# The first loads across all partitions, and the first memories through two PSUM banks

## The chip, the cores and the metric

The kernel runs on one core of a Trainium2 chip. Its engines work side by side: TensorE (PE) for matmuls, VectorE (DVE), ScalarE (ACT), GpSimd (POOL), and SyncE (SP), which only issues transfers. Transfers between HBM and the on-chip memory run on 16 DMA engines that all queues share; here SP's and ACT's queues issue them. The metric is the device time of one execution in microseconds (us).

## The reference

Attention over a compressed memory, then a feed-forward block with a squared ReLU. For 8 batches and 8 heads, with 576 tokens, 64 channels and 32 memory slots:

```python
a = exp(phi - max(phi, over tokens));  a = a / (sum(a, over tokens) + 1e-9)
k_m = einsum('bhsm,bhsd->bhmd', a, k)
v_m = einsum('bhsm,bhsd->bhmd', a, v)
scores = q @ k_m.T / sqrt(64)
attn = softmax(scores);  x = attn @ v_m       # tokens x (heads x channels) = 4608 x 512
h = maximum(x @ w_in, 0)                      # w_in: 512 x 2048, 8-byte floats
out = (h * h) @ w_out                         # w_out: 2048 x 512, 8-byte floats
```

Sums and maxima over tokens don't depend on the order of the tokens, as long as phi, k and v keep the same one.

## The kernel before

The attention output is never formed: `attn @ v_m @ w_in` is computed as `attn @ u` with `u = v_m @ w_in`, once per batch and part of `w_in`. The feed-forward matmuls split each operand into a high and a low part, and so run three products each (lines 673 to 679 and 724 to 731).

The eight heads are two groups of four (`qd` 0 and 1, `NQ` = 2). phi lies in HBM as 576 rows of 256 numbers (two groups of 4 heads x 32 slots), k and v as 576 rows of 4 heads x 128 numbers per group. On chip the tokens lie on 128 partitions: four full chunks of 128 tokens and a fifth of 64, the tail. `e_sb` holds phi and later its exponentials, chunk by chunk.

For batch 0 everything starts at once, in an order written out by hand: the list `loads` issues the transfers, and the string `order` in line 958 says which piece of work is recorded next (`e` phi's exponentials, `m` the memories k_m and v_m, `d0` to `d3` the decoding of `w_in` from 8-byte floats, `a0` and `a1` scores and softmax, `u0` the first u). Each engine runs its own instructions strictly in the order in which they were recorded. A transfer takes one of eight semaphores in turn (DMAHW0 to DMAHW7), and the issue of one that takes a semaphore again waits until its last user has landed.

The pieces that the change and the prediction's steps touch:

- `first_phi` (line 903) calls `load_phi(0)`: chunks 0 to 3 on SP's queue, the 64-row tail on ACT's. `first_kv` (line 884) loads k and v of each group as two transfers of two chunks (`u_hi3` and `u_lo3`, `wo4` and `wo5`: rooms lent from later use) and a tail of 64 rows.
- `exp_phi` (line 166): DVE takes the maximum over chunks (L170, L175), TensorE transposes it (L180), DVE reduces (L185), TensorE spreads it (L190), DVE adds it (L199), ACT takes the exponential (L201).
- `memories` (line 322): DVE sums the exponentials (L332, L335), TensorE multiplies them with k and v, 20 matmuls per group (L350) and the sums (L357), DVE divides (L366 to L370), TensorE transposes (L377), DVE and ACT copy to `mem` one half of the partitions each (L385).
- `by_heads` (L408) makes the scores of `a0` from `mem`, then `first_softmax` (L487 to L519) runs on DVE and ACT; L497 is its exponential on ACT, L501 the sum after it. L677 are the first feed-forward matmuls.
- `decode` (L581, L584 on ACT; L586, L589, L594 on DVE; L601) turns pieces of `w_in` into 4-byte floats. `q` is loaded by L397, `w_in` by L568.
- `spin` (L149) issues matmuls whose result nobody reads; they keep TensorE going while it waits.

Of the kernel before, what the change touches and what calls it, by code (L numbers as in the profile page):

```python
# [8 lines left out]
F32 = mybir.dt.float32  # L9
# [3 lines left out]
AF = mybir.ActivationFunctionType  # L13
# [11 lines left out]
def attn_moe_kernel(ctx: ExitStack, tc: tile.TileContext, qT, kv, phi, w_in, w_out, outT):  # L25
# [16 lines left out]
    P = 128  # L42
# [16 lines left out]
    def rows(c):  # L59
        return min(P, S - c * P)  # L60
# [51 lines left out]
    def fill_all():  # L112
        for c in range(NCH):
            fill(c, kvb[c])
            if rows(c) < P:
                nc.gpsimd.memset(e_sb[rows(c):, c], 0.0)

    ones = const.tile([P, CW - 2 * D], F32, name="ones")
    nc.gpsimd.memset(ones, 1.0)
# [33 lines left out]
    def load_phi(b, nc_q=nc.sync):  # L153
        nfull = S // P
        assert b == 0 or ("read", b - 1) in ready
        nc.sync.dma_start(out=e_sb[:, :nfull], in_=phi[b, :nfull * P].rearrange("(c p) x -> p c x", p=P))
        if b > 1:
            for qd in range(NQ):
                nc_q.dma_start(
                    out=e_sb[D * qd:D * (qd + 1), nfull, :P], in_=phi[b, nfull * P:, qd * P:(qd + 1) * P]  # L160
                )
            return [e_sb[:, c] for c in range(nfull)] + [e_sb[:, nfull, :P]]
        nc_q.dma_start(out=e_sb[:rows(nfull), nfull], in_=phi[b, nfull * P:])
        return [e_sb[:rows(c), c] for c in range(NCH)]

    def exp_phi(b, e):

        w = NQ * P
        mx = one.tile([P, w], F32, name="phi_mx")
        nc.vector.tensor_tensor(out=mx, in0=e[0], in1=e[1], op=ALU.max)  # L170
        for x in e[2:]:
            n = x.shape[0]
            if fine and not starting:
                yield True
            nc.vector.tensor_tensor(out=mx[:n], in0=mx[:n], in1=x, op=ALU.max)  # L175
        yield
        ps = new_ps()
        tp, bc = bank(ps, 0), bank(ps, 1)
        for qd in range(NQ):
            nc.tensor.transpose(tp[:, qd * P:(qd + 1) * P], mx[:, qd * P:(qd + 1) * P], ident)  # L180
        if starting:
            spin(1, ident, k=2)
        yield
        nmx = work.tile([P, NQ], F32, name="nmx")
        nc.vector.tensor_reduce(  # L185
            out=nmx, in_=tp[:, :w].rearrange("p (q x) -> p q x", q=NQ), axis=AX.X, op=ALU.max, negate=True
        )
# [24 lines left out]

    def exp_phi_blocks(b, e):

        w = NQ * P
        nb = w // M
        mx = one.tile([P, w], F32, name="phi_mx")
        nc.vector.tensor_tensor(out=mx, in0=e[0], in1=e[1], op=ALU.max)
        for x in e[2:-1]:
            nc.vector.tensor_tensor(out=mx, in0=mx, in1=x, op=ALU.max)  # L220
        at = [(slice(D * qd, D * (qd + 1)), slice(P * qd, P * (qd + 1))) for qd in range(NQ)]
        for hs, cs in at:
# [17 lines left out]
        for hs, cs in at:  # L240
            nc.vector.tensor_tensor(out=e[-1][hs], in0=e[-1][hs], in1=mx[hs, cs], op=ALU.subtract)
        yield
        nfull = S // P
        nc.scalar.activation(e_sb[:, :nfull], e_sb[:, :nfull], AF.Exp)
        nc.scalar.activation(e[nfull], e[nfull], AF.Exp)
        ready.add(("phi", b))

    def load_kv(b, qd, lent=None):

        got = []  # L250
        for c in range(NCH):
            if lent:
                t = lent(c)
            elif qd and b > 1 and rows(c) < P:
                nc.sync.dma_start(out=kvb[c][D:, :, :2 * D], in_=kv[b, qd, c * P:])
                got.append(kvb[c])
                continue
            elif qd:

                name, bufs = ("tmp", 3) if c < 3 else ("low", 2)  # L260
                if b == 2 and c < 3:
                    if not c:
                        w1 = const.tile([P, 3, 4, CW], F32, name="w1")
                    t = w1[:, c]
# [10 lines left out]
            nc.sync.dma_start(out=t[:rows(c), :, :2 * D], in_=kv[b, qd, c * P:c * P + rows(c)])  # L275
            got.append(t)
        return got

# [43 lines left out]
    def memories(b, e, kvs, mem):  # L322
# [7 lines left out]
        if b == 0:  # L330
            total = one.tile([P, NQ * P], F32, name="phi_mx")
            nc.vector.tensor_tensor(out=total, in0=e[0], in1=e[1], op=ALU.add)  # L332
            for c in range(2, NCH):
                n = rows(c)
                nc.vector.tensor_tensor(out=total[:n], in0=total[:n], in1=e[c][:n], op=ALU.add)  # L335
# [33 lines left out]
        for qd in range(NQ):  # L369
# [3 lines left out]
                den[:, qd:qd + 1],  # L373
            )
        yield
        for i in range(2 * NQ):
            nc.tensor.transpose(  # L377
                tp[:, i * P:(i + 1) * P], kvn[:, i // NQ, i % NQ].rearrange("p a d -> p (a d)"), ident
            )
        if starting:  # L380
            spin(1, ident, k=3)
        yield
        for half, copy in ((0, nc.vector.tensor_copy), (1, nc.scalar.copy)):
            hs = slice(D * half, D * (half + 1))
            copy(mem[hs], tp[hs].rearrange("p (x r h m) -> p x r h m", x=2, r=NPAIR, h=2)[:, :, :, half])  # L385
        done_ps(ps)
        ready.add(("mem", b))

# [495 lines left out]
    def first_kv(qd):

        names = (("u_hi3", "u_lo3", "u_hi4"), ("wo4", "wo5", "wo6"))[qd]
        queues = ((nc.scalar, nc.sync, nc.scalar), (nc.sync, nc.sync, nc.scalar))[qd]
        got = []
        for name, nc_q in zip(names, queues):
            c = len(got)  # L890
            t = const.tile([P, 2, 4, 2 * D], F32, name=name)
            n = min(2, S // P - c)
            if n:
                x = kv[0, qd, c * P:(c + n) * P].rearrange("(c p) h x -> p c h x", p=P)
                nc_q.dma_start(out=t[:, :n], in_=x)
                got += [t[:, k] for k in range(n)]
            else:
                fill(c, t[:, 0])
                nc_q.dma_start(out=t[:rows(c), 0], in_=kv[0, qd, c * P:])
                got.append(t[:, 0])  # L900
        kvs[qd] = got
# [5 lines left out]
    def next_kv():  # L907
# [1 line left out]

    loads = [  # L910
        (first_phi,),
        (first_kv, 0),
        (first_kv, 1),
        (fetch_w_in, 0, 0),
        (task_q, 0, 0),
        (task_q, 0, 1),
# [314 lines left out]
```

## Time and profile before

| | us |
|---|---|
| median of 3 runs | 719.02 (718.85 to 719.22) |
| span of the profiled execution, first to last instruction | 717.0 |
| TensorE busy | 708.0 (99% of the span) |
| VectorE busy | 388.6 (54%) |
| ScalarE busy | 332.6 (46%) |
| GpSimd busy | 197.6 (28%) |

The profiled execution has no time of its own beside its span; the runs' median is 2.0 us above that span, which stands for what lies before the first and after the last instruction. Busy TensorE counts the `spin` matmuls too. The DMA engines are almost fully busy in the first three of the page's 40 slices (to 54 us) and far less in most of the others. In the rows "idle before" names what an engine stood waiting for; "SPq" and "ACTq" are the queues of instructions that issue transfers, q1 and q10 the packets that came from them. A time to landing runs from the start of the issue.

### The profile page before, as it was taken

What the parts mean: (1) busy time and instruction counts of PE and PEld (TensorE: products, weight loads), DVE (VectorE), ACT (ScalarE), POOL (GpSimd) and SP (SyncE); (2) the same over time, 40 slices, a digit from 0 to 9 for tenths busy, and PEclk for the clock granted to TensorE, in tenths of its full rate; (3) what the DMA queues carried; (4) which work ended last, traced back from release to release, by engine and by line L of the source; (5) the groups of instructions that cost most, each with busy time, mean ns of one, the idle gap of its engine ahead of it and who ended that gap; (6) DMA issues with size and microseconds to landing.
All of it is one profiled execution on the core that took longest, in us unless ns stands there. A gap on an engine that the chain in (4) does not pass through costs nothing.

```text
span 717.0 us, 13710 instructions
## 1 busy us (share of the span) xinstructions
PE 708.0 (99%) x5380; PEld 617.4 (86%) x5380; DVE 388.6 (54%) x835; ACT 332.6 (46%) x644; POOL 197.6 (28%) x221
## 2 busy tenths in 40 slices
PE   9899999999999999999999999999999999999998
PEld 4477798987989998888999999888899899888997
DVE  4978787987686644445472645533573445221211
ACT  2648887875454443323442444323454244332332
POOL 1222103012320133222332334222433243223332
PEclk9999999999999999999999999999999999999999
DMA  9992435331876712083411911146221222100101
GB/s 305 390 351 93 147 138 139 123 122 37 253 243 217 199 59 69 28 230 120 147 59 43 306 69 37 59 145 171 94 89 67 90 96 96 59 1 1 59 1 37
DMA packets 63281, 89.50 MB, mean 125 GB/s; under 512 B 3888, under 2 KB 52272, under 8 KB 59632
## 3 DMA queue, kind: packets, MB, share of 16 engines
q1 hardware_dynamic: 62416, 87.52, 37.9%
q10 hardware_dynamic: 800, 1.10, 0.5%
q8 instruction: 42, 0.69, 0.4%
q14 instruction: 23, 0.19, 0.1%
HBM read 74.97 MB, written 13.63 MB: 124 GB/s over the span
## 4 chain that ended last, share of the span: by engine, by line
PE 93%; DMA 2%; DVE 2%; ACT 1%; issue 0%; POOL 0%; ACTq 0%; SPq 0%; DVEq 0%
PE acc L728 53%; PE h L677 28%; PE ps_m L408 5%; PE acc L720 3%; PE h L286 2%; DMA wo<-in_w_in 1%; DMA u_hi<-in_kv 1%; PE h L408 1%; PE h L149 1%; PE ps_m L350 0%; POOL a_lo L472 0%; DVE at L468 0%; DVE st L465 0%; DVE sm L454 0%; DVE u_lo L560 0%
## 5 line engine op out<-in xcount | busy, mean ns | idle before, releaser
L685 ACT ACTIVATE r_room<-h 128x320 f32<-128x320 f32 (+2 forms) x200 | 95.4, 477 | 262.9 <-PE h L677 256.9
L691 DVE TENSOR_TENSOR g_room<-h,r_room 128x320 f32<-128x320 f32 (+1 forms) x148 | 82.5, 558 | 238.7 <-ACT r_room L685 229.7
L728 PE MATMUL acc<-g_hi,wo 128*128 128x320 f32 (+1 forms) x1024 | 175.5, 308 | 0.0
L728 PEld LDWEIGHTS acc<-g_hi,wo 128*128 128x128 f32 x1024 | 155.6, 188 | 6.1 <-ACT r_room L685 2.5
L705 POOL TENSOR_TENSOR g_lo<-g_room,g_hi 128x320 fp32r<-128x320 f32 (+1 forms) x102 | 89.9, 882 | 223.9 <-DVE g_room L691 166.6
L728 PE MATMUL acc<-o,wo 128*128 128x512 f32 x576 | 139.9, 391 | 0.0
L728 PEld LDWEIGHTS acc<-o,wo 128*128 128x128 f32 x576 | 105.2, 188 | 21.5 <-issue 1.7
L677 PE MATMUL h<-a_hi,u_hi 128*128 128x320 f32 (+1 forms) x448 | 100.9, 306 | 0.7 <-ACT u_hi L558 0.7
L705 POOL TENSOR_TENSOR o<-g_room,o 128x512 fp32r<-128x512 f32 x48 | 62.0, 1291 | 143.7 <-PE acc L728 97.0
L728 PE MATMUL acc<-g_lo,wo 128*128 128x320 f32 (+1 forms) x512 | 100.7, 307 | 0.0
L677 PE MATMUL h<-a_hi,u_lo 128*128 128x320 f32 (+1 forms) x448 | 96.3, 296 | 0.8 <-DVE u_lo L560 0.8
L677 PE MATMUL h<-a_lo,u_hi 128*128 128x320 f32 (+1 forms) x448 | 96.1, 296 | 0.1
L677 PEld LDWEIGHTS h<-a_hi,u_hi 128*128 128x128 f32 x448 | 74.8, 189 | 23.6 <-DVE st L428 9.2
L728 PEld LDWEIGHTS acc<-g_lo,wo 128*128 128x128 f32 x512 | 81.5, 188 | 0.0
L677 PEld LDWEIGHTS h<-a_hi,u_lo 128*128 128x128 f32 x448 | 72.0, 189 | 1.9 <-DVE u_lo L560 1.9
L677 PEld LDWEIGHTS h<-a_lo,u_hi 128*128 128x128 f32 x448 | 72.2, 189 | 0.4 <-POOL a_lo L472 0.4
L701 ACT ACTIVATE g_hi<-r_room 128x320 fp32r<-128x320 f32 (+1 forms) x128 | 59.8, 467 | 7.6
L701 ACT ACTIVATE o<-r_room 128x512 fp32r<-128x512 f32 x48 | 30.4, 633 | 42.4 <-PE acc L728 42.0
L560 DVE TENSOR_TENSOR u_lo<-ps_m,u_hi 128x1024 fp32r<-128x1024 f32 (+1 forms) x29 | 34.3, 1183 | 4.6 <-ACT u_hi L558 4.1
L408 PE MATMUL ps_m<-w,mem 64*32 64x512 f32 (+1 forms) x528 | 35.6, 582 | 0.9 <-POOL w L601 0.9
L720 PE MATMUL acc<-g_hi,wo 128*128 128x256 f32 (+1 forms) x128 | 34.1, 409 | 0.0
L720 PEld LDWEIGHTS acc<-g_hi,wo 128*128 128x128 f32 x128 | 23.2, 190 | 7.0 <-issue 2.0
(175 smaller groups left out, 716.4 us busy)
## 6 DMA issues: line engine op xcount, KB each, us to landing
w<-w_f SPq DMA_DIRECT2D x24, 1024.0 KB, 4.8
wo<-in_w_in SPq DMA_DIRECT2D x16, 512.0 KB, 8.1
wo<-in_w_out SPq DMA_DIRECT2D x16, 512.0 KB, 8.0
kvb<-in_kv SPq DMA_DIRECT2D x28, 256.0 KB, 6.3
q_sb<-in_q SPq DMA_DIRECT2D x16, 320.0 KB, 6.2
out_t<-o SPq DMA_DIRECT2D x30, 160.0 KB, 1.9
e_sb<-in_phi SPq DMA_DIRECT2D x8, 512.0 KB, 6.9
w_f<-w SPq DMA_DIRECT2D x4, 1024.0 KB, 5.7
```

The lines of the kernel that those rows point to most:

```text
L149: nc.tensor.matmul(h[:, :k * P], x, ident[:, None, :].broadcast_to([P, k, P]), start=True, stop=True)
L286: nc.tensor.matmul(acc[qd][M * j:M * (j + 1), :CW], e_sb[hs, c, col + M * j:col + M * (j + 1)], kvs[qd][c][hs, j, :], start=(c == 0), stop ...
L408: nc.tensor.matmul(out[half][M * pr:M * (pr + 1), :y.shape[-1]], mem[hs, x, pr], y, start=True, stop=True)
L560: nc.vector.tensor_tensor(out=u_lo[:, :, n0:n1], in0=ps[:, :, :n1 - n0], in1=u_hi[:, :, n0:n1].bitcast(F32), op=ALU.subtract)
L677: nc.tensor.matmul(h[:, at:at + n], u[:, qd, fs], x[:, qd], start=(i == 0), stop=(i == len(todo) - 1))
L685: nc.scalar.activation(r, h[:, :T], AF.Relu)
L691: nc.vector.tensor_tensor(out=g, in0=h[:, :T], in1=r, op=ALU.mult)
L701: nc.scalar.activation(g_hi, r, AF.Square)
L705: adder.tensor_tensor(out=g_lo, in0=g, in1=g_hi.bitcast(F32), op=ALU.subtract)
L720: nc.tensor.matmul(acc[e][:, :T], wo[f][:, e * P:(e + 1) * P], g_hi, start=first, stop=last)
L728: nc.tensor.matmul(acc[e][:, :T], wo[f][:, w, e * P:(e + 1) * P], x, start=first and x is g_hi and w == 0, stop=last and x is g_lo,)
```

## The change

For batch 0 phi comes as two transfers of 128 rows: partition p takes tokens 4p to 4p+3, of which SP's queue loads the first two and ACT's the others. The 64 rows of the tail become a tile of 128 partitions, the first group of heads on the lower half and the second on the upper; k and v do the same, with one tail tile for both groups. The full chunks of k and v keep the same order of tokens, and so do the later batches' loads. DVE's maximum takes two chunks at once, and the tail's maximum, subtraction and exponential are done in two halves; the two unused quarters of the tail in `e_sb` are set to zero. One opening `spin` is taken out. The transposes of the first k_m and v_m write into two banks of another PSUM tile, and DVE copies k_m while ACT copies v_m, each in two halves.

```diff
     def load_phi(b, nc_q=nc.sync):
...
-        nc.sync.dma_start(out=e_sb[:, :nfull], in_=phi[b, :nfull * P].rearrange("(c p) x -> p c x", p=P))
+        x = phi[b, :nfull * P].rearrange("(p c) x -> p c x", p=P)
+        if b == 0:
+            for i, q in enumerate((nc.sync, nc_q)):
+                q.dma_start(out=e_sb[:, 2 * i:2 * i + 2], in_=x[:, 2 * i:2 * i + 2])
+            tail = one.tile([P, P], F32, name="at")
+            nc.sync.dma_start(out=tail, in_=phi[b, nfull * P:].rearrange("t (q x) -> q t x", q=NQ))
+            return [e_sb[:, c] for c in range(nfull)] + [tail]
+        nc.sync.dma_start(out=e_sb[:, :nfull], in_=x)
...
     def exp_phi(b, e):
...
+        if b == 0:
+            two = one.tile([P, 2, w], F32, name="st")
+            nc.vector.tensor_tensor(out=two, in0=e_sb[:, 0:2], in1=e_sb[:, 2:4], op=ALU.max)
+            nc.vector.tensor_tensor(out=mx, in0=two[:, 0], in1=two[:, 1], op=ALU.max)
+            for hs, cs in halves:
+                nc.vector.tensor_tensor(out=mx[hs, cs], in0=mx[hs, cs], in1=e[-1][hs], op=ALU.max)
...
+            if x.shape[-1] < w:
+                for hs, cs in halves:
+                    nc.vector.tensor_tensor(out=x[hs], in0=x[hs], in1=bc[hs, cs], op=ALU.add)
+                    nc.scalar.activation(e_sb[hs, NCH - 1, cs], x[hs], AF.Exp)
+                continue
...
+    def tokens_of(b, qd, c):
+        nfull = S // P
+        if c == nfull:
+            return kv[b, qd, c * P:]
+        return kv[b, qd, :nfull * P].rearrange("(p c) h x -> p c h x", p=P)[:, c]
...
+        two = new_ps(True) if starting else None
+        tps = [bank(two, i) for i in range(2)] if two is not None else [tp, tp[:, NQ * P:]]
         for i in range(2 * NQ):
+            x, qd = i // NQ, i % NQ
             nc.tensor.transpose(
-                tp[:, i * P:(i + 1) * P], kvn[:, i // NQ, i % NQ].rearrange("p a d -> p (a d)"), ident
+                tps[x][:, qd * P:(qd + 1) * P], kvn[:, x, qd].rearrange("p a d -> p (a d)"), ident
             )
...
+            for x, copy in ((0, nc.vector.tensor_copy), (1, nc.scalar.copy)):
+                for half in range(2):
+                    hs = slice(D * half, D * (half + 1))
+                    copy(mem[hs, x], tps[x][hs, :NQ * P].rearrange("p (r h m) -> p r h m", r=NPAIR, h=2)[:, :, half])
+            done_ps(two)
...
+    def first_kv():
+
+        nfull = S // P
+        tail = const.tile([P, 4, 2 * D], F32, name="u_hi4")
+        nc.scalar.dma_start(out=tail, in_=kv[0, :, nfull * P:])
+        for qd, names in enumerate((("u_hi3", "u_lo3"), ("wo4", "wo5"))):
+            x = kv[0, qd, :nfull * P].rearrange("(p c) h x -> p c h x", p=P)
+            got = []
+            for i, (nc_q, name) in enumerate(zip((nc.scalar, nc.sync), names)):
+                t = const.tile([P, 2, 4, 2 * D], F32, name=name)
+                nc_q.dma_start(out=t, in_=x[:, 2 * i:2 * i + 2])
+                got += [t[:, k] for k in range(2)]
+            kvs[qd] = got + [tail]
...
     spin(3, ident)
-    spin(1, ident, k=2)
```

ACT's instructions at the start of the program, before; the sizes behind the names are partitions x elements, and the number behind a room's name is that of its buffer.

```order
L163 DMA e_sb<-in_phi 64x256
L895 DMA u_hi_105<-in_kv 128x2x512
L899 DMA u_hi_109<-in_kv 64x512
L899 DMA wo_116<-in_kv 64x512
L942 ACT_TABLE_LOAD
L942 ACTIVATE ones<-ones 1x1 [waits Pool_49]
L201 ACTIVATE e_sb<-e_sb 128x256 [waits DMAHW1_49,DVE_49]
L201 ACTIVATE e_sb<-e_sb 128x256 [waits DVE_49] x3
L201 ACTIVATE e_sb<-e_sb 64x256 [waits DVE_49]
```

And after:

```order
L160 DMA e_sb<-in_phi 128x512
L926 DMA u_hi_108<-in_kv 128x1x512
L932 DMA u_hi_110<-in_kv 128x1024
L932 DMA wo_114<-in_kv 128x1024
L974 ACT_TABLE_LOAD
L974 ACTIVATE ones<-ones 1x1 [waits Pool_49]
L225 ACTIVATE e_sb<-e_sb 128x256 [waits DMAHW1_49,DVE_49]
L225 ACTIVATE e_sb<-e_sb 128x256 [waits DVE_49]
L225 ACTIVATE e_sb<-e_sb 128x256 [waits DMAHW0_49,DVE_49]
L225 ACTIVATE e_sb<-e_sb 128x256 [waits DVE_49]
L221 ACTIVATE e_sb<-at 64x128 [waits DMAHW3_49,DVE_49]
L221 ACTIVATE e_sb<-at 64x128 [waits DVE_49]
```

ACT's queue now carries half of phi, the tail of both groups of k and v, and two bulk transfers in place of one and three tails.

SP's instructions at the same place, before:

```order
L156 DMA e_sb<-in_phi 128x4x256
L895 DMA u_lo_107<-in_kv 128x2x512
L895 DMA wo_112<-in_kv 128x2x512
L895 DMA wo_114<-in_kv 128x2x512
L568 DMA wo_119<-in_w_in 128x512 [waits DMAHW0_49]
L397 DMA q_sb<-in_q 128x2x320 [waits DMAHW1_49]
L397 DMA q_sb<-in_q 128x2x320 [waits DMAHW2_49]
L397 DMA a_hi_124<-in_q 128x2x256 [waits DMAHW3_49]
L397 DMA a_lo_125<-in_q 128x2x256 [waits DMAHW4_49]
L568 DMA wo_128<-in_w_in 128x512 [waits DMAHW5_49]
L568 DMA wo_130<-in_w_in 128x512 [waits DMAHW6_49]
```

And after:

```order
L160 DMA e_sb<-in_phi 128x512
L162 DMA at<-in_phi 128x1x128
L932 DMA u_lo_112<-in_kv 128x1024
L932 DMA wo_116<-in_kv 128x1024
L606 DMA wo_118<-in_w_in 128x512 [waits DMAHW0_49]
L435 DMA q_sb<-in_q 128x2x320 [waits DMAHW1_49]
L435 DMA q_sb<-in_q 128x2x320 [waits DMAHW2_49]
L435 DMA a_hi_123<-in_q 128x2x256 [waits DMAHW3_49]
L435 DMA a_lo_124<-in_q 128x2x256 [waits DMAHW4_49]
L606 DMA wo_127<-in_w_in 128x512 [waits DMAHW5_49]
L606 DMA wo_129<-in_w_in 128x512 [waits DMAHW6_49]
```

SP carries two bulk transfers of k and v in place of three, and phi's tail. The semaphores belong to other transfers: DMAHW2, for which the second `q_sb` waits, was `u_hi` with its two chunks and is now the tail of k and v; DMAHW6, for which the third `w_in` piece (`wo_130`, now `wo_129`) waits, was a tail and is now `wo4`.

DVE around the copies to `mem`, before:

```order
L370 TENSOR_SCALAR st<-acc_174,den 128x2x128 [waits DVE_49]
L370 TENSOR_SCALAR st<-acc_174,den 128x2x128
L586 TENSOR_SCALAR tmp<-tmp 128x512 [waits Activation_49]
L589 TENSOR_SCALAR tmp<-tmp 128x512 [waits DVE_49]
L385 COPY mem<-acc_175 64x256 [waits PE_49]
L594 SCALAR_TENSOR_TENSOR tmp<-wo_119,tmp 128x512 [waits DMAHW0_49,DVE_49]
L487 STREAM_TRANSPOSE st<-acc_248 128x320 [waits PE_49]
L487 STREAM_TRANSPOSE st<-acc_249 128x320 [waits PE_49]
```

And after:

```order
L398 TENSOR_SCALAR st<-acc_174,den 128x2x128 [waits DVE_49]
L398 TENSOR_SCALAR st<-acc_174,den 128x2x128
L624 TENSOR_SCALAR tmp<-tmp 128x512 [waits Activation_49]
L627 TENSOR_SCALAR tmp<-tmp 128x512 [waits DVE_49]
L422 COPY mem<-ps_m 64x128 [waits PE_49]
L422 COPY mem<-ps_m 64x128
L632 SCALAR_TENSOR_TENSOR tmp<-wo_118,tmp 128x512 [waits DMAHW0_49,DVE_49]
L525 STREAM_TRANSPOSE st<-acc_251 128x320 [waits PE_49]
L525 STREAM_TRANSPOSE st<-acc_252 128x320 [waits PE_49]
```

DVE's one copy of 64 x 256 became two of 64 x 128, from the tile `ps_m`; ACT's copy became the other two.

## Rows read from the trace of the kernel before

**Rows 1.** The page's chain that ended last: share of the span by engine
```profile
PE 93%; DMA 2%; DVE 2%; ACT 1%; issue 0%; POOL 0%; ACTq 0%; SPq 0%; DVEq 0%
```

**Rows 2.** The chain in order of time, 0 to 60 us: start, length, what
```profile
11.48 8.96 DMA wo<-in_w_in
...
20.46 0.69 ACT tmp L581
21.15 0.56 ACT low L584
...
22.09 0.89 DVE sm L501 x2
...
28.80 1.73 PE h L677 x10
```

**Rows 3.** Timeline, 0 to 26 us: start, length, engine, line, what, count [idle before]
```profile
1.36 6.19 PE L149 MATMUL h<-ident 128*128 128x512 f32 x8 [1.36 <-POOL ones L119]
...
5.39 0.42 DVE L170 TENSOR_TENSOR phi_mx<-e_sb 128x256 f32<-128x256 f32 x1 [5.39 <-DMA e_sb<-in_phi]
...
5.85 1.34 DVE L175 TENSOR_TENSOR phi_mx<-phi_mx,e_sb 128x256 f32<-128x256 f32 x3
...
7.39 0.38 PE L180 MATMUL acc<-ident,phi_mx 128*128 128x128 f32 x2
...
8.84 1.88 PE L149 MATMUL h<-ident,nmx 128*128 128x512 f32 x4
...
10.65 0.64 PE L350 MATMUL acc<-u_hi,e_sb 128*32 128x128 f32 x16
...
11.76 1.32 PE L350 MATMUL acc<-wo,e_sb 128*32 128x128 f32 x40
...
13.01 0.61 PE L357 MATMUL acc<-ones,phi_mx 128*128 128x2 f32 x4
...
15.92 0.42 DVE L385 COPY mem<-acc 64x256 f32<-64x256 f32 x1 [0.19 <-PE acc L377]
...
16.37 0.37 ACT L385 COPY mem<-acc 64x256 f32<-64x256 f32 x1 [1.63 <-DVE mem L385]
...
16.46 0.83 PE L408 MATMUL acc<-q_sb,mem 64*32 64x320 f32 x9
...
20.94 0.69 DVE L594 SCALAR_TENSOR_TENSOR tmp<-wo,tmp 128x512 int32<-128x512 int32 x1
...
21.55 0.64 PE L408 MATMUL ps_m<-w,mem 64*32 64x256 f32 x8
21.60 0.82 ACT L497 ACTIVATE st<-st 128x320 f32<-128x320 f32 x2
```

**Rows 4.** DMA view, 3 to 3.5 us: queue, packets, MB, share of 16 engines
```profile
q1 hardware_dynamic: 167, 0.17, 96.0%
```

**Rows 5.** DMA view, 5 to 5.5 us, SP's queue
```profile
q1 hardware_dynamic: 95, 0.19, 105.3%
```

**Rows 6.** DMA view, 11.75 to 12.5 us, SP's queue
```profile
q1 hardware_dynamic: 75, 0.31, 102.5%
```

**Rows 7.** DMA view, 37 to 37.5 us, SP's queue, k and v
```profile
q1 hardware_dynamic: 290, 0.15, 119.8%
```

**Rows 8.** DMA view, 6.5 to 7 us, ACT's queue (q10) and SP's (q1)
```profile
q10 hardware_dynamic: 53, 0.11, 58.7%
q1 hardware_dynamic: 42, 0.09, 46.0%
```

**Rows 9.** DMA view, issues from 0 to 3.2 us: KB each, us to landing
```profile
u_hi<-in_kv ACTq DMA_DIRECT2D x1, 512.0 KB, 8.2
```

**Rows 10.** DMA view, 9 to 9.5 us, all queues
```profile
DMA packets 74, 0.11 MB, mean 230 GB/s; under 512 B 18, under 2 KB 18, under 8 KB 74
```

**Rows 11.** Timeline, 24 to 50 us, two DVE operations of other sizes
```profile
33.40 0.68 DVE L449 TENSOR_TENSOR st<-st,mx 128x512 f32<-128x512 f32 x1
...
37.73 0.16 DVE L457 TENSOR_SCALAR sm<-sm 128x16 f32<-128x16 f32 x1
```

More of the change, by code (lines that the diff above doesn't have):

```diff
@@ L115, in fill_all @@
             if rows(c) < P:
-                nc.gpsimd.memset(e_sb[rows(c):, c], 0.0)
+                nc.gpsimd.memset(e_sb[D:, c, :P], 0.0)
+                nc.gpsimd.memset(e_sb[:D, c, P:], 0.0)
     ones = const.tile([P, CW - 2 * D], F32, name="ones")
@@ L155, in load_phi @@
         assert b == 0 or ("read", b - 1) in ready
-        nc.sync.dma_start(out=e_sb[:, :nfull], in_=phi[b, :nfull * P].rearrange("(c p) x -> p c x", p=P))
+        x = phi[b, :nfull * P].rearrange("(p c) x -> p c x", p=P)
[6 more added lines that the diff above has]
+        nc.sync.dma_start(out=e_sb[:, :nfull], in_=x)
+        if b == 1:
+            nc.gpsimd.memset(e_sb[D:, nfull, P:], 0.0)
         if b > 1:
@@ L164, in load_phi @@
         return [e_sb[:rows(c), c] for c in range(NCH)]
+    halves = [(slice(D * qd, D * (qd + 1)), slice(P * qd, P * (qd + 1))) for qd in range(NQ)]
     def exp_phi(b, e):
@@ L169, in exp_phi @@
         mx = one.tile([P, w], F32, name="phi_mx")
[L170 to L175, printed above, removed]
+        if b == 0:
[4 more added lines that the diff above has]
+                nc.vector.tensor_tensor(out=mx[hs, cs], in0=mx[hs, cs], in1=e[-1][hs], op=ALU.max)
+        else:
+            nc.vector.tensor_tensor(out=mx, in0=e[0], in1=e[1], op=ALU.max)
+            for x in e[2:]:
+                n = x.shape[0]
+                if fine and not starting:
+                    yield True
+                nc.vector.tensor_tensor(out=mx[:n], in0=mx[:n], in1=x, op=ALU.max)
         yield
@@ L220, in exp_phi_blocks @@
             nc.vector.tensor_tensor(out=mx, in0=mx, in1=x, op=ALU.max)
-        at = [(slice(D * qd, D * (qd + 1)), slice(P * qd, P * (qd + 1))) for qd in range(NQ)]
-        for hs, cs in at:
+        for hs, cs in halves:
             nc.vector.tensor_tensor(out=mx[hs, cs], in0=mx[hs, cs], in1=e[-1][hs], op=ALU.max)
@@ L239, in exp_phi_blocks @@
             nc.vector.tensor_tensor(out=x, in0=x, in1=mx, op=ALU.subtract)
-        for hs, cs in at:
+        for hs, cs in halves:
             nc.vector.tensor_tensor(out=e[-1][hs], in0=e[-1][hs], in1=mx[hs, cs], op=ALU.subtract)
@@ L274, in load_kv @@
                 nc.gpsimd.memset(t[rows(c):, :, 2 * D:], 1.0)
-            nc.sync.dma_start(out=t[:rows(c), :, :2 * D], in_=kv[b, qd, c * P:c * P + rows(c)])
+            nc.sync.dma_start(out=t[:rows(c), :, :2 * D], in_=tokens_of(b, qd, c))
             got.append(t)
@@ L332, in memories @@
             nc.vector.tensor_tensor(out=total, in0=e[0], in1=e[1], op=ALU.add)
-            for c in range(2, NCH):
-                n = rows(c)
-                nc.vector.tensor_tensor(out=total[:n], in0=total[:n], in1=e[c][:n], op=ALU.add)
+            for x in e[2:]:
+                nc.vector.tensor_tensor(out=total, in0=total, in1=x, op=ALU.add)
         for qd, kvt in kvs.items():
@@ L382, in memories @@
         yield
-        for half, copy in ((0, nc.vector.tensor_copy), (1, nc.scalar.copy)):
-            hs = slice(D * half, D * (half + 1))
-            copy(mem[hs], tp[hs].rearrange("p (x r h m) -> p x r h m", x=2, r=NPAIR, h=2)[:, :, :, half])
+        if two is None:
+            for half, copy in ((0, nc.vector.tensor_copy), (1, nc.scalar.copy)):
+                hs = slice(D * half, D * (half + 1))
+                copy(mem[hs], tp[hs].rearrange("p (x r h m) -> p x r h m", x=2, r=NPAIR, h=2)[:, :, :, half])
+        else:
+            for x, copy in ((0, nc.vector.tensor_copy), (1, nc.scalar.copy)):
+                for half in range(2):
+                    hs = slice(D * half, D * (half + 1))
+                    copy(mem[hs, x], tps[x][hs, :NQ * P].rearrange("p (r h m) -> p r h m", r=NPAIR, h=2)[:, :, half])
+            done_ps(two)
         done_ps(ps)
@@ L882, in attn_moe_kernel @@
     kvs = {}
[L884 to L901, printed above, removed]
+    def first_kv():
[10 more added lines that the diff above has]
+            kvs[qd] = got + [tail]
     def first_phi():
@@ L911, in attn_moe_kernel @@
         (first_phi,),
-        (first_kv, 0),
-        (first_kv, 1),
+        (first_kv,),
         (fetch_w_in, 0, 0),
```

## The prediction

> **What bounds the kernel now.** I read the shares of the chain first, then the chain in order of time, then the timeline of the first 30 us, then the DMA view in narrow stretches. TensorE holds 93% of the chain [rows 1], and the change touches nothing of that stretch. So the question is when the first real matmuls of the feed-forward part start, since every later one follows at the same distance. In order of time the chain before them is a wait for a transfer of `w_in` that ends at 20.43 us, two ACT passes over it, the exponential queued behind them on ACT, and then DVE's softmax from 22.09 us up to the first feed-forward matmuls at 28.80 [rows 2]. Ahead of that, in the timeline, stands the path that the change rewrites: phi is there at 5.39, DVE takes its maximum until 7.19, the transposes start at 7.39, the filler matmuls of 8.84 hold TensorE until 10.65, when the products with k and v begin; those end at 13.0, the memory is copied from 15.92 to 16.74, the scores start at 16.46 [rows 3]. Two paths thus meet at 22.09: the transfers through ACT, and DVE, whose own work was done at 20.94 + 0.69 = 21.63. If only one of them gets shorter, the other takes over, DVE 0.46 us below the present.
>
> **The new loads.** In the order before the change ACT's queue carries small tails, and SP's the bulk; after it ACT carries half of phi, the tail of both groups of k and v, and half of the rest, SP the other half. What one packet costs one of the 16 DMA engines follows from packets and share in a stretch: 16 x 0.5 us x 0.960 / 167 = 46 ns for 1 KB [rows 4], 89 ns for 2 KB [rows 5], 164 ns for 4 KB (16 x 0.75 x 1.025 / 75) [rows 6], 33 ns for 512 B [rows 7]. Phi's 512 packets are 32 per engine, 1.47 us, and DVE starts on them at 5.39; so 3.92 us are start and completion, and a transfer lands at 3.92 plus the packets ahead of it on its slowest engine. With both queues full an engine takes from them about in turn (53 packets of one, 42 of the other) [rows 8]. Test: `u_hi` of before has phi 1.47, its tail 0.18, `u_lo` 1.42, itself 1.42 and as much of SP's next beside it, 5.9 in all, so 9.8; issued at 1.34 it landed 8.2 later, at 9.5 [rows 9].
>
> The phi tail and the k,v tail are the only transfers in either program whose source begins with a count of two (two blocks of 64 rows); all others begin with 64 rows or more. What that does, no row of before shows. From one side: the 64 + 64 rows are dealt to all 16 engines, 8 each, and the k,v tail costs each 8 x 89 = 0.71 us. From the other: the transfer is dealt out by its outer count, one block to one engine, and two engines carry 64 packets each, 64 x 89 = 5.68 us, and 64 x 33 = 2.11 us for the phi tail. I take the second, with doubt. What speaks for it in the trace is that the shape of a transfer, and not its bytes alone, decides how the engines serve it: with the two 64-row tails of before under way the rate is 230 GB/s [rows 10], where 2 KB packets at 89 ns make 369.
> The Trainium skill, "DMA: Bandwidth & Descriptors", section "Why a DMA increments its semaphore by 16 and not by 1", says that a transfer uses the largest number of engines up to 16 that divides the outermost count of both its sides. No run here shows one with an outermost count below 64; by that rule both tails go to two engines and the sum is the 724.8 below, against 718.1 without it.
>
> Then, on those two engines, ACT's queue is half of phi 0.71, the k,v tail 5.68, `u_hi` 8 x 164 = 1.31, `wo4` 1.31: 9.01. SP's beside it is half of phi 0.71, the phi tail 2.11, `u_lo` 1.31, `wo5` 1.31: 5.44. So `wo4` lands at 3.92 + 9.01 + 5.44 = 18.4; at 12.9 if ACT's queue went first, at 19.7 if a `w_in` piece (1.31) gets between. The phi tail, packet about packet with the k,v tail, lands near 3.92 + 1.42 + 64 x 0.122 = 13.1, and DVE's maximum ends 13.7 where it ended 7.19: that alone moves the products from 10.65 to 17.2, and `wo4` is wanted 1.1 us after their start, at 18.3. Both paths agree; 1.25 us from the first `wo` row to the row of L357 (11.76 to 13.01) puts L357 at 18.4 + 1.25 = 19.65, **6.64 later**.
>
> What SP issues behind waits too: each of its loads waits for the one eight before it, so the second q piece now waits for the k,v tail, the last q piece for `u_hi`, and the third `w_in` piece for `wo4` at 18.4. Behind that issue lie at most 1.31 (first `w_in`), 1152 KB of q (128 x 2 x 320 twice and 128 x 2 x 256 twice, in four bytes; 36 packets of 2 KB per engine, 3.2) and two `w_in` pieces (2.62): 25.5, and ACT's two passes 1.25: 26.8. The exponential is wanted at 27.4 by DVE's path (below, less 0.5), so this stays hidden by about 0.6.
>
> **DVE and ACT before the products.** Four maxima, 0.42 + 1.34 [rows 3], become one of 128x512, one of 128x256 and two of 64x128. For 128x512 there is 0.68; for 64x128 I bound by 0.16 (128x16) and 0.42 and take 0.29, near the middle [rows 3, 11]: 0.68 + 0.42 + 0.58 = 1.68, from 1.42 to 1.94. No gain and no loss. The adds and exponentials of the tail, two halves for one op, cost some 0.2 us more, and the tail's products come 0.9 us after the first ones: hidden. The last sum takes 128 rows for 64, at the same columns: nothing. The POOL memsets that go stood beside waits of others. The opening filler that goes ended at 7.4 to 7.55, the transposes started at 7.39, DVE was done at 7.19: 0.2 at most, and it is nothing where phi's tail is late.
>
> **The copies.** Before: DVE 15.92 to 16.34, then ACT 16.37 to 16.74, and the scores of the upper half wait for ACT. After: DVE copies k_m alone, two of 64x128 (0.56, from 0.32 to 0.84), with the first two transposes done 0.2 earlier; ACT's v_m is wanted only by the products of 21.55 [rows 3]. Gain 0.35, from -0.05 to 0.6.
>
> **The sum.** L357 +6.64, copies -0.35, and the 0.46 that DVE stood waiting for ACT goes: +5.83. The profiled span is 717.0; some 2.0 us around it make the median of 719.02. 717.0 + 5.8 + 2.0 = **724.8 us**, its own range 721 to 726.5 (`wo4` at 14.5 to 19.7). Later batches' phi and k,v come in another order of rows, under a TensorE that is 99% busy: nothing.
>
> **Rivals.**
> *The tails spread over all 16 engines.* Then an engine's whole list is 2 x 0.71 + 0.26 + 0.71 + 4 x 1.31 = 7.64, everything lands by 11.6; by the same count before it is 1.47 + 0.18 + 72 x 0.089 = 8.04, 12.0, and the slow stretch of the 64-row tails, two to three half-microseconds at 230 GB/s, goes too: 0.4 to 1.1 sooner, so the `w_in` piece of 20.43 lands near 19.5. DVE's side gives 0.46 + 0.35 and up to 0.2. The smaller decides: about -0.9, **718.1**, from 717.3 to 718.9. This is the case on the other side; it decides from the point where `wo4` lands before 11.7. Against it: the source's two blocks; for it: every transfer in the trace is served by all engines. It becomes a measurable gain (beyond 1.44) only if both paths give nearly their most.
> *Spread, but TensorE starts slow.* The opening fillers take 6.19 us for eight matmuls, the later ones 1.88 for four [rows 3], so the engine begins at 1.2 GHz and reaches 2.4 only by about 7.4, with no pause before. After, the fillers end near 6.5 and it stands idle until about 7. If it then stays at the lower level, the two fillers of 8.84 take 1.88 us more and hold the products: +1.9 - 0.9, **720.0**. The page's clock line shows nines all along, so the trace gives the durations alone.
> *Only part of it bites:* ACT's queue is served first on the two engines, `wo4` at 12.9, L357 at 14.2: +1.1 - 0.6, 719.5.
>
> **Chances.** Two engines 0.63 (724.8); spread 0.29 (718.1), 0.08 of it faster beyond 0.2%; slow start 0.04; ACT first 0.04. What can be told from no change is 0.2%, 1.44 us. Slower 0.63, same 0.29, faster 0.08. The range 717.6 to 726.3 takes in both main cases and leaves 0.1 to 0.15 outside; the likeliest one's own is 721 to 726.5.
>
> **What would show it.** In the new profile: the landing of the k,v tail near 12 to 14 and of `wo4` near 18, a DMA share far below 1 between 10 and 18 us with packets still moving (two of 16 engines), DVE's small maximum waiting for the phi tail, the row of L357 near 19.6, the scores 0.35 nearer to it than before, no wait of L501 on ACT. Wrong if the tails land with the rest by 12, if the share stays at 1, or if the first feed-forward matmuls stand at 28 us or before.

## The result, and the profile after

The changed kernel takes **727.97 us** (726.38 to 728.77, 4 runs), the kernel before in the same session 719.08 (718.85 to 719.22): ratio 1.0122, 95% interval 1.0108 to 1.0137. It is 8.9 us slower, where 5.8 were forecast; the profiled execution has a span of 726.7 us for 717.0, so 9.7.

TensorE has lost part of its share of the chain, to DMA above all [rows 1]:

```profile
PE 88%; DMA 5%; DVE 4%; SPq 1%; ACT 1%; issue 0%; POOL 0%; DVEq 0%; ACTq 0%
```

The timeline of the start, columns as in [rows 3], in two answers (0 to 45 us, and 20 to 60 for the last rows):

```profile
1.36 5.28 PE L150 MATMUL h<-ident 128*128 128x512 f32 x6 [1.36 <-POOL ones L120]
...
5.22 0.42 DVE L185 TENSOR_TENSOR phi_mx<-st 128x256 f32<-128x256 f32 x1
...
14.55 0.60 DVE L187 TENSOR_TENSOR phi_mx<-phi_mx,at 64x128 f32<-64x128 f32 x2 [8.90 <-DMA at<-in_phi]
...
17.21 3.24 PE L150 MATMUL h<-ident,nmx 128*128 128x512 f32 x4
...
20.39 0.64 PE L378 MATMUL acc<-u_hi,e_sb 128*32 128x128 f32 x16
...
22.71 0.61 PE L385 MATMUL acc<-ones,phi_mx 128*128 128x2 f32 x4
...
25.61 0.61 DVE L422 COPY mem<-ps_m 64x128 f32<-64x128 f32 x2 [0.20 <-PE ps_m L408]
...
26.15 0.89 PE L446 MATMUL acc<-q_sb,mem 64*32 64x320 f32 x16
...
31.04 0.87 DVE L539 TENSOR_REDUCE sm<-st 128x10 f32<-128x320 f32 x2
...
31.27 1.26 POOL L639 TENSOR_TENSOR w<-tmp,low 128x512 int32<-128x512 int32 x1 [2.86 <-DVE tmp L632]
31.94 0.62 DVE L541 TENSOR_SCALAR sm<-sm 128x20 f32<-128x20 f32 x1
...
38.17 0.56 PE L715 MATMUL h<-a_hi,u_lo 128*128 128x320 f32 x2 [0.64 <-DVE u_lo L598]
```

DVE has the maximum of the four full chunks at 5.64 and then waits 8.90 us for the phi tail. The ones products (the sums, L357 before and L385 now), at 13.01 before [rows 3], stand at 22.71, 9.70 later, and the end of the span moves by as much. From them to the end it is 703.99 us in both profiles (717.0 - 13.01, 726.7 - 22.71): the whole loss is made before that row, and behind it the gains and losses even out.

The DMA view of the loads issued from 0 to 3.2 us (KB each, median us from issue to landing; compare [rows 9]) shows which transfers are odd. For the two tails it has no landing at all, and those that queue behind them take 12 to 16 us:

```profile
u_lo<-in_kv SPq DMA_DIRECT2D x1, 512.0 KB, 15.0
u_hi<-in_kv ACTq DMA_DIRECT2D x1, 512.0 KB, 12.3
wo<-in_kv SPq DMA_DIRECT2D x1, 512.0 KB, 15.7
wo<-in_kv ACTq DMA_DIRECT2D x1, 512.0 KB, 14.5
e_sb<-in_phi ACTq DMA_DIRECT2D x1, 256.0 KB, 3.7
...
u_hi<-in_kv ACTq DMA_DIRECT2D x1, 256.0 KB
at<-in_phi SPq DMA_DIRECT2D x1, 64.0 KB
```

The trace behind this view also keeps the times at which each transfer reports to its semaphore. The other six transfers of the view report sixteen times. Each of the two tails reports three times: once 1.3 us after its issue began, and twice at its end, at 13.12 and 13.14 us for k and v and at 14.29 and 14.46 for phi. Of the sixteen reports of ACT's `u_hi` fourteen come between 7.83 and 9.98 us and the last two at 14.60 and 14.64; of ACT's `wo` fourteen by 13.27 and two at 17.14 and 17.16. Read as one report per engine, fourteen engines were done with each load some 4 us earlier, and two held it back.

The view by stretches (us, then the busy time of PE, PEld, DVE, ACT and POOL, the granted clock, the DMA share, GB/s) shows the second loss. TensorE is idle from 6.64, and its granted clock goes from 2.4 to 1.2 GHz in the 8 to 10 row; it has the full level back only in the 20 to 22 row:

```profile
6.00:8.00 2.00, 0.64 (x1) 0.00 (x0) 0.00 (x0) 0.00 (x0) 0.00 (x0) 1.00 0.99 313
8.00:10.00 2.00, 0.00 (x0) 0.00 (x0) 0.00 (x0) 0.00 (x0) 0.00 (x0) 0.93 1.04 314
10.00:12.00 2.00, 0.00 (x0) 0.00 (x0) 0.00 (x0) 0.00 (x0) 0.00 (x0) 0.50 1.03 298
...
18.00:20.00 2.00, 2.00 (x4) 0.67 (x2) 1.83 (x7) 1.95 (x7) 0.00 (x0) 0.51 0.92 246
20.00:22.00 2.00, 2.00 (x61) 1.61 (x64) 1.22 (x3) 1.15 (x2) 0.00 (x0) 1.00 0.96 364
```

The mean over the span is 0.993, for 1.000 before. The fillers of 17.21 take 3.24 us for 1.88 before [rows 3], and the products queue behind them. The granted clock also reads 1.00 in the opening, but the weight loads of the fillers there begin 0.85 us apart (4.08, 4.93), as they do at 0.50 (18.07, 18.92) and not as behind the products (23.69, 24.12, so 0.43). By that pace TensorE had not yet worked at full speed when the wait began.

### The profile page after: what moved, and what is told of

Its sections match the earlier page's. It is cut to its first block, busy times and chain, and to the rows that moved or that the text cites. A ratio compares the mean times of both kernels' runs of the same rounds, so it can differ in the third digit from the quotient of the medians.

```text
span 726.7 us, 13714 instructions
## 1 busy us (share of the span) xinstructions
PE 709.3 (98%) x5378; PEld 618.0 (85%) x5378; DVE 389.8 (54%) x837; ACT 333.1 (46%) x646; POOL 196.9 (27%) x221
## 4 chain that ended last, share of the span: by engine, by line
PE 88%; DMA 5%; DVE 4%; SPq 1%; ACT 1%; issue 0%; POOL 0%; DVEq 0%; ACTq 0%
PE acc L766 50%; PE h L715 27%; PE ps_m L446 4%; PE acc L758 3%; DMA wo<-in_kv 2%; PE h L315 2%; DMA wo<-in_w_out 1%; DMA wo<-in_w_in 1%; PE h L446 1%; SPq L304 1%; DVE wo L698 1%; DMA u_hi<-in_kv 0%; DVE tmp L624 0%; DVE tmp L632 0%; PE ps_m L378 0%
## 5 line engine op out<-in xcount | busy, mean ns | idle before, releaser
L446 PE MATMUL ps_m<-w,mem 64*32 64x512 f32 (+1 forms) x528 | 35.6, 582 | 0.9 <-POOL w L639 0.9
L758 PE MATMUL acc<-g_hi,wo 128*128 128x256 f32 (+1 forms) x128 | 34.1, 409 | 0.0
L758 PEld LDWEIGHTS acc<-g_hi,wo 128*128 128x128 f32 x128 | 23.2, 189 | 7.0 <-issue 2.0
```

The costliest lines, as they stand in the source:

```text
L446: nc.tensor.matmul(out[half][M * pr:M * (pr + 1), :y.shape[-1]], mem[hs, x, pr], y, start=True, stop=True)
L758: nc.tensor.matmul(acc[e][:, :T], wo[f][:, e * P:(e + 1) * P], g_hi, start=first, stop=last)
```

## The experiments

All ratios are against the kernel before, run beside each. "Tails split" means two transfers of 64 rows, one per group, for one transfer of two blocks.

**Is it the source of two blocks? Its cause alone, in the kernel before.**

```diff
-   nc_q.dma_start(out=t[:rows(c), 0], in_=kv[0, qd, c * P:])
+   x = kv[0, qd, c * P:].rearrange("(t a) h x -> a t h x", a=2)
+   nc_q.dma_start(out=t[:rows(c), 0], in_=x)
    (the first phi tail alike; in the control a=16)
```

> The kernel before, with nothing of the change, but its three first tails of 64 rows (phi, and k,v of both groups) read even tokens first and odd tokens second, so that each source begins with a count of two (2 blocks of 32 rows); rows, bytes, packet sizes and queues are the same, and the sum over tokens is the same. Theory (a source that begins with a count of two is carried by two of 16 engines): an engine with tails has 32 packets of 1 KB and 64 of 2 KB where it had 2 and 8, some 1.4 us for phi and 5 us for k,v more; the ones products (L357) move from 13.0 to 18 to 21 us, TensorE loses its clock on the way, and the time is 724 to 729. Rival (another part of the change delayed the tails): 718.7 to 719.5, as before.

> The same edit of the kernel before, with the tokens of each tail dealt into 16 blocks of 4 rows, so that each source begins with a count of 16: the control for the run with two blocks. Theory (the outer count decides): 16 engines carry it and the time is that of before, 718.7 to 719.6. Rival (rows out of order in memory, not the outer count, are what is slow): as slow as with two blocks, 724 or more.

Two blocks: 730.78 us (730.41 to 730.94), ratio 1.0160 (1.0144 to 1.0175). Sixteen blocks: 718.80, ratio 0.9995 (0.9985 to 1.0005). The same rows, bytes, data packets and queues cost 11.7 us or nothing, by the outer count alone. The number of engines stands in the DMA view from 0 to 26 us, in the line of ACT's queue (packets, MB, share), here with two blocks and then with sixteen:

```profile
q10 hardware_dynamic: 470, 0.85, 9.5%
```

```profile
q10 hardware_dynamic: 512, 0.85, 9.8%
```

By the sizes in the trace 448 of them are the same data in both runs (64 of 1 KB, 384 of 2 KB). The rest are packets of 4 bytes: 64 in the control, sixteen for each of the queue's four transfers, and 22 with two blocks, which is sixteen for the one unedited transfer and two for each of the three edited ones. The DMA view of the two-block run has no landing for just the three edited transfers, and in the timeline the products stand and wait for two of them:

```profile
u_hi<-in_kv ACTq DMA_DIRECT2D x1, 512.0 KB, 8.3
u_hi<-in_kv ACTq DMA_DIRECT2D x1, 128.0 KB
wo<-in_kv ACTq DMA_DIRECT2D x1, 128.0 KB
e_sb<-in_phi ACTq DMA_DIRECT2D x1, 64.0 KB
```

```profile
16.79 0.58 PE L351 MATMUL acc<-u_hi,e_sb 128*32 128x128 f32 x8 [4.49 <-DMA u_hi<-in_kv]
...
21.91 0.66 PE L351 MATMUL acc<-wo,e_sb 128*32 128x128 f32 x8 [2.84 <-DMA wo<-in_kv]
22.49 1.02 PE L358 MATMUL acc<-ones,phi_mx 128*128 128x2 f32 x4
```

In the control the same view has them landing as any other:

```profile
u_hi<-in_kv ACTq DMA_DIRECT2D x1, 128.0 KB, 7.8
wo<-in_kv ACTq DMA_DIRECT2D x1, 128.0 KB, 8.1
e_sb<-in_phi ACTq DMA_DIRECT2D x1, 64.0 KB, 4.3
```

**Undone in the changed kernel: both tails, the k,v tail, the phi tail.**

```diff
-   nc.sync.dma_start(out=tail, in_=phi[b, nfull * P:].rearrange("t (q x) -> q t x", q=NQ))
+   for qd in range(NQ):
+       nc.sync.dma_start(out=tail[D * qd:D * (qd + 1)], in_=phi[b, nfull * P:, qd * P:(qd + 1) * P])
-   nc.scalar.dma_start(out=tail, in_=kv[0, :, nfull * P:])
+   for qd in range(NQ):
+       nc.scalar.dma_start(out=tail[D * qd:D * (qd + 1)], in_=kv[0, qd, nfull * P:])
```

> The changed kernel, with each of the two tails loaded as two transfers of 64 rows instead of one transfer of two blocks. Theory (a transfer whose source begins with a count of two is carried by two of the 16 DMA engines, and that is the whole loss): the k,v tail lands by 10 us instead of 13.1, the phi tail by 7 instead of 14.4, the ones products (L385 in the changed kernel) stand near 13 instead of 22.7, and the time is 717.5 to 719.5, level with before. Rival (the new order of rows, with runs of 4 KB, or the heavier ACT queue is what makes the loads late): the tails land a little sooner, but the time stays at 724 to 728.

> Only the k,v tail as two transfers of 64 rows; the phi tail still as one of two blocks. Theory, with the phi tail's landing as what decides: its 64 packets on each of two engines now take turns with packets of 4 KB instead of 2 KB, it lands at 12 to 14 us instead of 14.4, the ones products stand at 20.5 to 22.5, and the time is 725.5 to 728. Rival (the k,v tail and wo4 behind it decide, as the prediction had them on equal terms): 718.5 to 721.

> Only the phi tail as two transfers of 64 rows; the k,v tail still as one of two blocks. Theory: DVE has its phi by 7 us and the products with k and v could start near 10.7, but the k,v tail lands at 12 to 13.5 and wo4 behind it at 14 to 17, so that the ones products stand at 15.5 to 18 and the time is 721 to 724. Rival (only the phi tail matters, the k,v tail is hidden behind the bulk): 718 to 719.5.

With the phi tail split, L379, L386 and L447 are the lines L378, L385 and L446 of the changed kernel. Both split: 720.18 us (719.48 to 723.73, 12 runs), ratio 1.0024 (1.0012 to 1.0035). Most of the loss is gone (8.9 to 1.2 us), somewhat more than expected stays. Only the k,v tail split: 722.22, 1.0049 (1.0031 to 1.0067), between the two expectations, in two groups of runs: 720.1 to 721.0 at a mean clock of 0.999 or more, 723.4 to 725.0 at 0.995. Only the phi tail split: 727.83, 1.0125 (1.0106 to 1.0145): my expectation of 721 to 724 failed, and the rival of 719 more so. The k,v tail alone costs as much as both: `u_hi` stands behind it in ACT's queue, the tail's last report comes at 15.04 us and that of `u_hi` at 16.28, and the products wait for it until 16.41. This run also shows the two engines bare, since SP's next loads have not started yet: from 14 to 16 us the DMA share is 0.13, two sixteenths, while ACT's queue has packets to serve all along. The same view as above, and the timeline:

```profile
14.00:16.00 2.00, 0.00 (x0) 0.00 (x0) 0.43 (x1) 1.21 (x2) 0.00 (x0) 0.86 0.13 52
16.00:18.00 2.00, 1.59 (x32) 1.62 (x36) 0.00 (x0) 0.00 (x0) 0.00 (x0) 0.50 0.91 279
...
24.00:26.00 2.00, 2.00 (x7) 0.96 (x6) 0.00 (x0) 0.00 (x0) 0.00 (x0) 0.58 1.02 410
```

```profile
16.41 1.08 PE L379 MATMUL acc<-u_hi,e_sb 128*32 128x128 f32 x16 [3.43 <-DMA u_hi<-in_kv]
...
20.84 1.02 PE L386 MATMUL acc<-ones,phi_mx 128*128 128x2 f32 x4
21.71 3.76 PE L150 MATMUL h<-ident 128*128 128x512 f32 x4
...
26.64 0.89 PE L447 MATMUL acc<-q_sb,mem 64*32 64x320 f32 x16
```

**How much of it is the clock?** More fillers, so that TensorE is busy while it waits; the late transfers stay.

```diff
-   spin(3, ident)
+   spin(4, ident)           # phi tail split; 6 with the k,v tail split; 11 and 13 in the changed kernel
-   spin(2, nmx[:, :1].broadcast_to([P, P]))
+   spin(7, nmx[:, :1].broadcast_to([P, P]))     # phi tail split only
```

> The changed kernel with the phi tail as two transfers of 64 rows (the k,v tail still of two blocks), as measured at 727.8, with one more filler ahead of the transposes and five more ahead of the products with k and v, so that TensorE is busy while it waits for u_hi. Theory (the wait costs little by itself, the half clock after it some 4 us): granted clock 1.0 through 16 to 26 us, products to scores in 5.8 to 6.5 us where the run without the fillers took 10.2, time 723 to 724.5. Rival (the late transfers alone make the 727.8): 726.5 to 728.5.

> The changed kernel with the k,v tail as two transfers of 64 rows (the phi tail still of two blocks); its runs fell into two groups, 720.1 to 721.0 at a mean clock of 0.999 or more and 723.4 to 725.0 at 0.995. Here with three more fillers ahead of the transposes. Theory (the groups differ only by whether TensorE's clock falls before the phi tail is there): all runs in the lower group, 720 to 721.3, clock 0.999 or more. Rival (the groups come from the transfers, and the clock follows): runs in both groups still.

Phi tail split, with fillers: 724.70 us (724.31 to 724.82), 3.1 less than without, ratio to before 1.0075 (1.0060 to 1.0090). `u_hi` is as late, the clock is whole, and from the first products to the scores it is 5.9 us (16.44 to 22.30) for 10.2:

```profile
14.00:16.00 2.00, 1.53 (x4) 0.38 (x2) 0.00 (x0) 1.11 (x2) 0.00 (x0) 1.00 0.13 52
16.00:18.00 2.00, 1.56 (x56) 1.44 (x60) 0.00 (x0) 0.11 (x1) 0.00 (x0) 1.00 0.88 268
```

```profile
16.44 0.64 PE L379 MATMUL acc<-u_hi,e_sb 128*32 128x128 f32 x16 [0.91 <-DMA u_hi<-in_kv]
...
18.85 0.61 PE L386 MATMUL acc<-ones,phi_mx 128*128 128x2 f32 x4
```

K,v tail split, with fillers: 721.13 (720.66 to 722.44), 1.0031 (1.0020 to 1.0042), clock 0.999 or more in all seven runs. The upper group has gone, but two runs at a whole clock stand at 722.4, so the clock is not all of the scatter. That the rest is the landing (last section) is likely, but these two runs have no profile.

> The changed kernel with both tails still late, and eight more filler matmuls in front of the transposes, so that TensorE does not stand idle from 6.6 us until the phi tail is there at 14.4. Theory (part of the loss is TensorE at half clock when the phi tail arrives): the granted clock stays at 1.0 through 8 to 20 us, the stretch from the transposes to the first products takes 3.3 us as before instead of 5.5, the ones products stand at 20.3 to 20.9 instead of 22.7, and the time is 2 us lower, 725 to 726.5. Rival (DVE and ACT set that stretch, the clock costs nothing): same as the changed kernel, 727 to 728.5.

> The changed kernel once more, unaltered, as what the run with longer fillers is set against: 726.4 to 728.8 as in its first four runs, mean clock 0.992 to 0.994 in all of them.

> The changed kernel with ten more fillers ahead of the transposes, which hold TensorE until about 16 us, where eight ended at 14.06 and left runs with a mean clock of 0.995 and 728.7 to 730.2 beside two at 0.999 and 726.4 to 727.0. Theory (the half clock is about 2 of the 8.9 us that the change costs, the late tails the rest): clock 0.999 or more in nearly all runs, and 726.0 to 727.0, 1 to 2 us under the changed kernel run beside it; what the fillers overrun the phi tail by, up to 1 us, is taken off the gain. Rival (the clock costs nothing here): level with the changed kernel, 727 to 729.

Eight more fillers in the changed kernel: 727.85 (726.41 to 730.17), 1.0132 (1.0115 to 1.0148). The changed kernel again: 728.22 (726.10 to 729.94), 1.0119 (1.0099 to 1.0139); ten more fillers: 727.91 (727.03 to 728.50), 1.0122 (1.0108 to 1.0136), at 1.000 in all runs. By the times this is a miss, nothing comes of the fillers. The profiles suggest why it can't be seen there. With ten:

```profile
16.03 0.60 DVE L187 TENSOR_TENSOR phi_mx<-phi_mx,at 64x128 f32<-64x128 f32 x2 [10.56 <-DMA at<-in_phi]
...
19.90 0.65 PE L378 MATMUL acc<-u_hi,e_sb 128*32 128x128 f32 x16
...
22.34 0.61 PE L385 MATMUL acc<-ones,phi_mx 128*128 128x2 f32 x4
```

From the end of the maximum to the products it is 3.27 us (16.63 to 19.90, and 15.57 to 18.84 with eight), where the changed kernel needs 5.24 (15.15 to 20.39) and, in its second profile, 4.20 (16.60 to 20.80): the clock costs 0.9 to 2.0 us. But DVE had the phi tail at 14.55 in the changed kernel's first profile, 14.97 with eight fillers, 16.00 in its second profile and 16.03 with ten; this scatter of 1.5 us can cover the gain in so few runs. The two profiles whose phi tail came at the same time (16.00 and 16.03) have spans of 726.9 us without and 726.2 with fillers.

**What of the rest of the change?** The copies alone in the kernel before; the copies and the new order of rows with the tails of before; the split tails on other queues.

```diff
    copies (both): task_mem as in the change, and for the second run also
-   .rearrange("(c p) x -> p c x", p=P)
+   .rearrange("(p c) x -> p c x", p=P)
    split tails on SP, or in the queues of before (both with spin(1, ident, k=2) put back):
-   nc.scalar.dma_start(out=tail, in_=kv[0, :, nfull * P:])
+   nc.sync.dma_start(out=tail[D * g:D * (g + 1)], in_=kv[0, g, nfull * P:])      # behind u_lo
-   zip((nc.scalar, nc.sync), names)
+   zip((nc.sync if qd else nc.scalar, nc.sync), names)      # wo4 to SP; tails stay on ACT, phi whole on SP
```

> The kernel before with only the new copies of the memory (two banks, each copied by one engine). Prediction's term: 0.35 us less, 718.4 to 718.8. What the changed kernel's profile shows from the first copy to the first transposition of the scores: 1.51 us for 1.71, 0.2 less. Rival (DVE is full from there on, nothing comes through): 718.9 to 719.3.

> The kernel before with two parts of the change alone: the new order of rows (tokens 4p to 4p+3 on partition p, so packets of 4 KB, in all batches) and the new copies of the memory. Its three tails, their queues and the eight first transfers are those of before. Theory (what left the three spread versions 1.2 to 2.0 us behind is that they have nine or ten first transfers where eight can be under way, so that the last is issued only when phi has landed): the bulk lands no later than before, 718.4 to 719.4. Rival (the order of rows or the copies cost it): 720 or more, as the spread versions.

> The changed kernel with both tails as two transfers of 64 rows each, the k,v tail's on SP's queue behind u_lo so that ACT's queue has only phi, u_hi and wo4, and the short opening filler of before put back. Theory (with 16 engines on every load the change is level with before; the 1.2 us that the first such version was slower is wo4 at 12.3 us at the end of ACT's queue, and now and then a lost clock): wo4 lands by 11.5, no wait between the products, clock 0.999 or more in all runs, 718.5 to 719.8. Rival (the spread version is slower by its own work, two small maxima that wait for two landings and one semaphore more per tail): 720 or more.

> The changed kernel with both tails as two transfers of 64 rows and the queues as before the change: ACT's queue has the phi tail, u_hi and the k,v tails, SP's has phi in one transfer, u_lo, wo4 and wo5 in that order; the short opening filler is put back. Theory (what left the first two spread versions 1.2 to 1.5 us behind is the sharing of the bulk between two queues, which makes both wo pieces and the second half of the phi tail land last, at 12.3 and at 6.9 to 8.6 us): DVE has its phi by 6.8, wo4 lands near 10.7, no wait between the products, and the time is 718.4 to 719.4, level with before. Rival (the row order, the small maxima and the copies cost it themselves): 720 or more, whatever the queues.

Copies alone: 719.18 us, ratio 1.0001 (0.9992 to 1.0009). Copies and row order: 719.02, ratio 1.0000 (0.9991 to 1.0009). So this half of the change is worth nothing either way. The split versions: 720.62, 1.0024 (1.0014 to 1.0035), and 721.03, 1.0035 (1.0021 to 1.0048); the expectations of both missed, and their rivals (720 or more) hold by the number. The profiles lose at different places. In the first split version the products wait 0.63 us for `wo`. With the tails on SP, DVE waits 2.12 us for the second half of the phi tail, the granted clock falls to 0.50, and the products wait for no load. In the last the products wait 2.01 us for a k,v tail (this profile is of a run of 724.29 us at a clock of 0.994; four of its six runs stand at 721.0 and 1.000):

```profile
2.61 2.83 ACTq L934 DMA_DIRECT2D u_hi<-in_kv  x2
...
13.88 0.42 PE L378 MATMUL acc<-u_hi,e_sb 128*32 128x128 f32 x8 [2.01 <-DMA u_hi<-in_kv]
```

The issue of those two tails lasts until 5.44: of the nine first transfers the ninth is issued at 4.97, when the first half of the phi tail has landed (4.95; each load waits for the one eight before it, as the prediction has it), and what it carries lands last. All three split versions have nine or ten first transfers, all versions that are level with before have eight. That fits; a split version with eight was not run, nor were the two small maxima, each of which waits for its own half of the phi tail, tried alone. So the number of transfers is not shown to be the cause of these 1.2 to 2.0 us. No version beat the kernel before.

## Why the prediction was right in kind and too low

**The mechanism** was right: two blocks, two engines, everything queued behind them late. The marks that it named and that came: the k,v tail lands at 13.1 (12 to 14 foretold), `wo4` at 17.2 (2.71 + 14.5; near 18), DVE's small maximum waits for the phi tail (8.90 us), no wait on ACT before the row of L539. Two did not come: L385 stands at 22.71 for 19.6, and the scores start 3.44 us behind it for 3.45 before, not 0.35 nearer. That the k,v tail alone is enough for the whole loss is shown by the 727.83 with the phi tail mended. The DMA share "far below 1 between 10 and 18 us" was hidden in the changed kernel by SP's next loads (0.82 to 0.84 from 12 to 18 us) and is bare in the run with the phi tail split, 0.13. What the prediction took from the trace for two engines, the 230 GB/s beside the 64-row tails of before, was no sign of them: both those tails have a landing in that kernel's view, from sixteen reports each, and 18 of the 74 packets there are under 512 B [rows 10].
By the Trainium skill, "DMA: Bandwidth & Descriptors", section "Why a DMA increments its semaphore by 16 and not by 1", a transfer takes the largest number of engines, up to 16, that divides the outermost count of both its sides; two blocks give two engines, sixteen blocks all of them. The two runs on the kernel before agree, 730.78 and 718.80 us, and so do their 4-byte packets, two and sixteen for a tail.

**The step that failed** is "that alone moves the products from 10.65 to 17.2". It has two mistakes. The phi tail was to be there at 13.1 and was at 14.55 (up to 16.03 in other profiles), so DVE's maximum ended at 15.15 for 13.7: 1.45. The tail of k and v did land at 13.1; that of phi came 1.3 later and so was not served packet about packet with it, and why is open. And the stretch from there to the products was carried over at its old length, 3.5 us, although the step itself left TensorE idle for 8 us: at half clock it took 5.24, 1.74 more. The slow start stood among the rivals, with a price of 1.9 us, but only for the case in which nothing is late; it belonged to the main sum, where the wait is longest. With 0.13 back behind the products, L385 is 9.70 later for 6.64, 3.06 more. Of the two paths that "agree" in the prediction only DVE's set the time: `wo4` landed at 17.2 for 18.4 and SP's last piece at 18.3, both before the products began at 20.39.
The run with the phi tail split and fillers has the k,v tail late and the clock whole, as the sum had it, and took 724.70 us for 724.8 predicted. That it agrees to 0.1 us is luck: its ones products stand at 18.85, 0.80 before the sum's 19.65, and the 0.81 of gains behind them is missing there too (its span ends 704.15 us later, for 703.99 before).

**Two gains did not arrive**, 0.81 together. The copies gave 0.20: from the first copy to DVE's first transposition of the scores it is 1.51 us (25.61 to 27.12) for 1.71 (15.92 to 17.63), of which nothing could be measured in the run with the copies alone. DVE's 0.46 went, as foretold, but the prediction did not say what is late next: the small L541, 0.18 us before (23.01), took 0.62 and ended at 32.56, with GpSimd's L639 (31.27 + 1.26 = 32.53). Before, it ended at 23.19, with GpSimd's 23.05. So 0.12 of the 0.46 was left. The other profiles agree: in the eleven where the 128x20 operation takes 0.43 or 0.62 us it ends 0.02 to 0.04 behind GpSimd's, the kernel before with two blocks among them, and in the other five it takes 0.17 or 0.18 and starts at most 0.14 before GpSimd's end. That GpSimd's operation holds it is read from these times, not tested. At the row of 38.17 the shift is 9.37 (28.80 before [rows 2]), 0.33 less than 9.70; in a group of second-layer matmuls that stood at 41.25 (L720) and now at 50.80 (L758) it is 9.55, and at the end of the span 9.70 again. Where these 0.33 went I have not found.
5.83 + 3.06 + 0.81 = 9.70.

**The rivals.** Loads over all 16 engines were priced at 718.1, 0.9 under before. No run has just that, since the split versions, 720.2 to 721.0, also make a ninth and a tenth transfer, which the rival had not to count. The copies and the row order on sixteen engines gave 719.02, no gain. "ACT queue first" did not occur.

## What to carry to other kernels

Look at the outermost count of a DMA's source as at its size: 2 instead of 64 cost 11.7 us here and 16 nothing, with the same bytes and data packets. When a step of a sum makes TensorE wait, price what follows at the lower clock as well. Fillers where the wait can't be removed gave 3.1 us in one version and nothing that the times show in another. After a wait that goes, name what ends beside it: here 0.34 of 0.46 us was lost again to the next operation.

## What else the runs showed

The landing of the same two-engine transfer is not steady in the changed kernel and its variants: DVE had the phi tail at 14.55 to 16.03 us, and beside a split k,v tail at 9.87 in one profile and 6.89 in another; the changed kernel's runs reach from 726.1 to 729.9. It is not so in each kernel that has such transfers: the kernel before with two blocks stayed within 0.53 us (730.41 to 730.94, 4 runs). Why, is open.

One split version shows how near the edge the opening is: in its twelve runs ten stood at 719.5 to 721.2 with a clock of 0.999 or more, two at 723.7 with 0.995.
